# Staging the first expert unit's weights while the attention still runs

## The chip, the cores and the metric

The kernel runs on one core of a Trainium2 chip. The metric is the time of one execution on the device in microseconds (us), the median of several runs. The engines are PE (matrix products), PEld (PE's weight loads), ACT, DVE and POOL (elementwise work), and SP, which only issues DMAs here; POOL issues some DMAs too. Every engine works off its own list of instructions in a fixed order, and a semaphore holds an instruction back until what it reads is there.

## The reference

Three stages follow one another. First a linear attention with a state, for 4 x 8 heads, 768 steps, head width 48:

```
for t in range(S):
    y[:, :, t] = q_t @ state
    state = state + b_t * k_t (x) (v_t - k_t @ state)        # k normalized
```

Its output, as x of 3072 tokens x 384, goes through a mixture of 8 experts. All experts see all tokens and are weighted by P, the softmax of x @ w_gate after 8 rounds of row and column normalization:

```
for e in range(8):
    out += P[:, e:e+1] * (maximum(x @ w1[e], 0) @ w2[e])     # w1: 384 x 1024, w2: 1024 x 384
```

A last stage computes (((x @ u1) * (x @ u2)) @ u3) @ u4. Everything is float32. The kernel gets there with pairs: each operand is split into a rounded high part and the remainder (hi and lo), and a product is three matmuls: hi hi, hi lo, lo hi.

## The kernel before, in words

Every operation is recorded in a plan (`Plan.op`) with its possible engines, a cost, what it reads and writes, and a priority; a smaller number goes first. `Plan.order` then simulates the engines with these costs and emits the program in the order that comes out. An operation that may run on POOL or DVE gets its engine there. The hardware follows that order per engine, and waits where data is late.

The attention runs in 12 chunks (`prep_k`, `invert`, `tt_make`, `prep_q`, `seq`). Expert 0 is computed beside it chunk by chunk (`e0`), from the weights in the eight slots of `wA`. On PE the last chunks of `e0` come after the end of the attention. The normalization of P (`sinkhorn`) runs on DVE between them, with a small PE product in each of its eight rounds.

Experts 1 to 7 follow in `phase_b`. Tokens are taken in three passes of 1024; in a pass every expert is done in two halves of 512 hidden features, so a pass has 14 units (`unit`), and a unit has two pairs q = 0, 1 of 128-feature blocks. The first product of a pair of blocks with two groups of tokens is done by a scheme of the Strassen kind, which needs, beside the blocks of w1 themselves, five sums and differences of them: S1 to S4, kept in the tile `wS`, and S5, kept in place of a block in `wA`. A unit has 66 such matmuls for the two pairs together (the steps of `STEPS`), and then 72 matmuls with w2 into six outputs (`m2`), each multiplied by P on DVE and added to the tile `acc` on POOL.

`load_pair` brings one pair in. In the first pass (p = 0) it loads the raw float32 rows of two blocks with four DMAs into the two buffers of `rawB` (ring `self.rawB`), splits each into hi (ACT) and lo (POOL or DVE) in the pair's two slots of `wA`, forms the five sums in place in `rawB` (`sub`), splits these into `wS` and `wA`, and writes the finished forms to DRAM with two DMAs (`wq_d`, `ws_d`). The later passes load those forms. The sums overwrite the raw rows, so they come after both splits of the raw rows; and since all pairs share the two buffers of `rawB`, the loads of the next pair come after the splits of the sums.

Two gates matter. `w1open` (prio -200) fires when the attention's preparation is done: `open_w1` frees the pool `prep` and opens `ident` and `rawB`. `bopen` fires when all of the attention is done: `open_b` frees its pools and opens `xT` (the tokens' forms), `acc`, `hB`, `wS` and others. The loads into `rawB` carry `r0`, the gate `w1open` and the gate `x11` (the attention's last chunk written to DRAM); the copy into `wS` carries `bopen`. The slots of `wA` that the first unit's pairs go to are 0 to 3, which `e0` reads until its last chunk. `phase_b` calls `load_pair` for the first unit with prio 390 and for unit n + 1 with prio 400.5 + n. `forms` makes the nine forms of a pass's tokens.

Of the kernel before, what the change touches and what calls it, by code (L numbers as in the profile page):

```python
# [6 lines left out]
F32 = mybir.dt.float32  # L7
F32R = mybir.dt.float32r
# [4 lines left out]
ALU = mybir.AluOpType  # L13
# [19 lines left out]
HB = 5  # L33
# [10 lines left out]
BB = 2.0  # L44
# [274 lines left out]
def pool2(n):  # L319
    return (2.2 * n + 70) / 1000  # L320
# [6 lines left out]
def actb(n):  # L327
    return (n / 1.2 + 155) / 1000


def dveb(n, pair=False):
    return (n * (1.25 if pair else 1.0) + 140) / 960


class Kernel:
# [533 lines left out]
            e, self.wb(n)[:, 768:1536], rv(), self.wb(n)[:, 0:768].bitcast(F32), ALU.subtract),  # L869
            r=[(raw, 0), (raw, 1), ("w", sl, 0)], w=[("w", sl, 1)], prio=prio)  # L870

    def load_pair(self, p, e_, h, q, prio):

        nc, g, T, a = self.nc, self.g, self.T, self.a
        r0 = ["w1open", "x11"]
        n1 = 8 * e_ + 4 * h + 2 * q
        ps = 2 * h + q
        wk = lambda n: [("w", n % 8, i) for i in range(2)]
        sk = [("wS", ps, i, m) for i in range(2) for m in range(2)]
        two = lambda: T["wA"][:, n1 % 8:n1 % 8 + 2].rearrange("p a n -> p (a n)")  # L880
        if p:
            self.dma(two, lambda: T["wq_d"][e_, ps], 1572864, [("wq", e_, ps)], wk(n1) + wk(n1 + 1), prio, eng="POOL")
            self.dma(lambda: T["wS"][:, ps], lambda: T["ws_d"][e_, ps], 524288, [("ws", e_, ps)], sk, prio, eng="POOL")
            return
        raws = []
        for j, n in enumerate((n1, n1 + 1)):
            f, sl = n % 8, n % 8
            raw = self.rawB.new()
            raws.append(raw)
            rv = lambda raw=raw: T["rawB"][:, raw.at]  # L890
            self.dma(lambda rv=rv: rv()[:, 0:384].rearrange("p (k f) -> p k f", k=3),
                     lambda f=f: a["moe_w1"][e_, :, 128 * f:128 * f + 128].rearrange("(k p) f -> p k f", p=128), 196608, r0, [(raw, 0)], prio)
            self.dma(lambda rv=rv: rv()[:, 384:768], lambda f=f: a["moe_w2"][e_, 128 * f:128 * f + 128, :], 196608, r0, [(raw, 1)], prio)
            c0 = 128 * j
            m = 768 - c0
            g.op({"ACT": actb(m)}, lambda e, n=n, rv=rv, c0=c0: self.copy("ACT", self.wb(n)[:, c0:768], rv()[:, c0:768]),
                 r=[(raw, 0), (raw, 1)], w=[("w", sl, 0)], prio=prio)
            g.op({"POOL": pool2(m), "DVE": BB * dveb(m, True)}, lambda e, n=n, rv=rv, c0=c0: self.tt(
                e, self.wb(n)[:, 768 + c0:1536], rv()[:, c0:768], self.wb(n)[:, c0:768].bitcast(F32), ALU.subtract),
                r=[(raw, 0), (raw, 1), ("w", sl, 0)], w=[("w", sl, 1)], prio=prio)  # L900
        r1, r2 = raws
        k = lambda raw, i: T["rawB"][:, raw.at, 128 * i:128 * i + 128]

        def sub(out, i0, i1, op, m=1):

            g.op({"POOL": pool2(128), "DVE": BB * dveb(128, True)}, lambda e: self.tt(e, k(*out), k(*i0), k(*i1), op), r=[], w=[(r1, 0), (r2, 0)], prio=prio)
        sl2 = (n1 + 1) % 8
        sub((r2, 1), (r2, 0), (r2, 1), ALU.add)
        sub((r2, 0), (r1, 0), (r2, 0), ALU.subtract)
        sub((r1, 0), (r2, 1), (r1, 0), ALU.subtract)  # L910
        sub((r1, 1), (r1, 1), (r1, 0), ALU.subtract)
        sub((r1, 2), (r1, 2), (r2, 2), ALU.subtract)
        ws = lambda i, c0=0: T["wS"][:, ps, 512 * i + c0:512 * i + c0 + 256]
        rk = [(r1, 0), (r2, 0)]
        for m, src, dst, key in ((256, lambda: T["rawB"][:, r1.at, 0:256], lambda i: ws(i), lambda i: ("wS", ps, i, 0)),
                                 (256, lambda: T["rawB"][:, r2.at, 0:256], lambda i: ws(i, 256), lambda i: ("wS", ps, i, 1)),
                                 (128, lambda: T["rawB"][:, r1.at, 256:384], lambda i: self.wb(n1 + 1)[:, 768 * i:768 * i + 128], lambda i: ("w", sl2, i))):
            g.op({"ACT": actb(m)}, lambda e, src=src, dst=dst: self.copy("ACT", dst(0), src()), r=rk + ["bopen"], w=[key(0)], prio=prio)
            g.op({"POOL": pool2(m), "DVE": BB * dveb(m, True)}, lambda e, src=src, dst=dst: self.tt(e, dst(1), src(), dst(0).bitcast(F32), ALU.subtract),
                 r=rk + [key(0)], w=[key(1)], prio=prio)  # L920
        self.dma(lambda: T["wq_d"][e_, ps], lambda: two().bitcast(F32), 1572864, wk(n1) + wk(n1 + 1), [("wq", e_, ps)], 1000)
        self.dma(lambda: T["ws_d"][e_, ps], lambda: T["wS"][:, ps].bitcast(F32), 524288, sk, [("ws", e_, ps)], 1000)

# [206 lines left out]
    def phase_b(self):  # L1130
        nc, g, T, a = self.nc, self.g, self.T, self.a
        self.rawB = Ring(range(2), fifo=True)

        def open_w1(e):
            self.close("prep")
            self.open("wBp", "right", ident=((128, 128), F32))
            self.open("rawp", "right", rawB=((128, 2, 768), F32))
        self.after("w1open", self.prep_ops, -200, open_w1)
        self.dma(lambda: T["ident"], lambda: a["ident"], 65536, ["w1open"], ["ident"], -100)
        self.sinkhorn()  # L1140
        self.after("x11", [g.wr["xs", 11, b] for b in range(2)], -200)

        def open_b(e):
            self.close("xst")
            self.close("seq")
            self.open("xTp", "left", xT=((128, 4, 2, 4, 3, 128), F32R))
            self.open("accp", "left", acc=((128, 2, 3, 512), F32))
            self.open("hBp", "right", hB=((128, HB, 1024), F32R), wS=((128, 4, 1024), F32R))
            self.open("cvp", "right", cv=((128, 3, CN), F32R), cvr=((128, 1, 2 * CN), F32), rt=((128, 4, 512), F32))
            self.open("pbp", "right", pb=((128, 2, 512), F32), tmp=((128, 2, 512), F32))  # L1150
        self.hringB = Ring([], fifo=True)
        self.rt = Ring([], fifo=True)

        def opened(end):
            self.hringB.free.extend([(end, i) for i in range(HA, HA + HB)])
            self.rt.free.extend([(end, i) for i in range(4)])
        self.after("bopen", self.seq_ops + self.prep_ops, -200, open_b, hook=opened)
        self.after("hA", self.e0_ops, -200, hook=lambda end: self.hringB.free.extend([(end, i) for i in range(HA)]))
        self.spread_p()
        units = [(p, e_, h) for p in range(3) for e_ in range(1, NE) for h in range(2)]  # L1160
        for n, (p, e_, h) in enumerate(units):
            pr = 400.0 + n
            if n == 0:
                for q in range(2):
                    self.load_pair(p, e_, h, q, 390)
            if (e_, h) == (1, 0):
                self.forms(p, pr - .6)
            if h == 0:
                pb = [self.pbring.new() for _ in range(2)]
                for s in range(2):  # L1170
                    self.dma(lambda s=s, pb=pb: T["pb"][:, pb[s].at], lambda s=s, e_=e_, p=p: T["p_d"][
                        e_, 512 * self.PASSES[p][s]:512 * self.PASSES[p][s] + 512].partition_broadcast(128), 262144, ["pd"], [pb[s]], pr - .4)
            if n + 1 < len(units):
                for q in range(2):
                    self.load_pair(*units[n + 1], q, pr + .5)
            self.unit(p, e_, h, pr, 250.0 + n / 100, pb)
            if n == NC0:
                self.after("cv0", [g.wr["acc", 0, 2]], 2)
            if (e_, h) == (4, 0):
                self.add_first(p, pr + .6)  # L1180
            if (e_, h) == (7, 1) and p < 2:
                for s, ch in enumerate(self.PASSES[p]):
                    self.dma(lambda ch=ch: T["xf_d"][ch], lambda s=s: T["acc"][:, s], 786432, [("acc", s, kk) for kk in range(3)], [("xf", ch)], 260 + n / 100)
# [300 lines left out]
```

## Time and profile before

| | us |
|---|---|
| time, median of 3 runs | 2138.53 (2131.8 to 2141.47) |
| the profiled execution's own time | 2133.49 |
| span of that execution, first to last instruction | 2131.3 |
| PE busy in it | 2034.6 (95%) |
| DVE, POOL, ACT busy | 1245.0, 843.3, 712.8 |

The profile is of one execution. Times in its rows are microseconds from the start of the span. A busy share says nothing about which engine sets the end in a stretch; for that the stretch itself is read, with what each engine waited for. L368 is the line of the helper that issues every two-input elementwise operation, L361 that of every copy on ACT, L357 that of the matmuls, L388 that of the DMAs, so the rows are told apart by their tiles; b is a PSUM bank, y_d and w_d stand for the DRAM tensors with a number in their name.

### The profile page before, as it was taken

The numbers are of one execution on the slowest core, as the hardware profiler recorded it, in microseconds if no ns is written. First come the engines' busy times: TensorE is split into PE (matmuls) and PEld (weight loads), VectorE is DVE, ScalarE is ACT, GpSimd is POOL, SyncE is SP. The second block draws the span as 40 slices with busy tenths as digits, with TensorE's granted clock in tenths as the row PEclk, the third lists the DMA queues.
The fourth block names the chain that finished last, engine by engine and source line by source line (L and its number), as shares of the span: only waits on it lengthen the run. The fifth ranks groups of instructions, "written<-read, shape, count | busy, mean of one in ns | idle before, by whom it ended". The sixth has DMA issues, their size and how long they took to land.

```text
span 2131.3 us, 39119 instructions
## 1 busy us (share of the span) xinstructions
PE 2034.6 (95%) x16017; PEld 1734.2 (81%) x16017; DVE 1245.0 (58%) x1950; ACT 712.8 (33%) x1384; POOL 843.3 (40%) x903
## 2 busy tenths in 40 slices
PE   2899999989999999999999999999999999999999
PEld 1798889968887788788887888788877888988888
DVE  7998883535445545757667667666667644222222
ACT  3543333234334344333233234233232232222222
POOL 3101100246676766735547545434555534200000
PEclk9899999999999999999999999999999999999999
DMA  6523332155556565766565555555565455510000
GB/s 215 160 83 109 97 99 73 53 190 214 187 189 202 189 216 197 252 218 213 177 212 187 186 191 197 198 202 193 177 219 186 163 167 174 113 34 27 16 18 27
DMA packets 165460, 331.60 MB, mean 156 GB/s; under 512 B 13280, under 2 KB 117664, under 8 KB 153760
## 3 DMA queue, kind: packets, MB, share of 16 engines
q1 hardware_dynamic: 131392, 193.82, 27.6%
q0 software_dynamic: 33888, 135.28, 18.8%
q8 instruction: 126, 2.06, 0.4%
q14 instruction: 54, 0.44, 0.1%
HBM read 235.10 MB, written 93.95 MB: 154 GB/s over the span
## 4 chain that ended last, share of the span: by engine, by line
PE 79%; DVE 7%; DMA 5%; POOL 4%; issue 3%; ACT 1%; SPq 1%; DVEq 0%; POOLq 0%; ACTq 0%
PE b L357 79%; DMA rawB<-in_moe_w 2%; DVE prod L368 1%; SPq L388 1%; POOL wA L368 1%; DMA kt<-in_kT 1%; POOL acc L368 1%; DVE cv L371 1%; POOL rawB L368 1%; POOL wS L368 1%; DVE b L368 1%; DVE hA L371 0%; DMA w_d<-cv 0%; DVE t L568 0%; DMA wA<-wq_d 0%
## 5 line engine op out<-in xcount | busy, mean ns | idle before, releaser
L357 PE MATMUL b<-hA,wA 128*128 128x512 f32 (+1 forms) x2367 | 505.4, 353 | 7.6 <-DVE hA L371 7.5
L357 PEld LDWEIGHTS b<-hA,wA 128*128 128x128 f32 x2367 | 390.9, 189 | 70.8 <-DVE hA L371 8.9
L368 POOL TENSOR_TENSOR acc<-acc,tmp 128x512 f32<-128x512 f32 x252 | 331.9, 1319 | 157.5 <-DVE tmp L368 153.5
L357 PE MATMUL b<-hB,wA 128*128 128x512 f32 x1521 | 389.4, 391 | 0.0
L357 PEld LDWEIGHTS b<-hB,wA 128*128 128x128 f32 x1521 | 287.6, 189 | 60.0
L357 PE MATMUL b<-xr,wA 128*128 128x256 f32 (+1 forms) x1620 | 331.0, 338 | 1.5 <-DVE a L371 1.3
L357 PEld LDWEIGHTS b<-xr,wA 128*128 128x128 f32 x1620 | 252.8, 191 | 34.5 <-DVE a L371 1.4
L368 DVE TENSOR_TENSOR tmp<-b,pb 128x512 f32<-128x512 f32 x234 | 161.0, 689 | 204.2 <-PE b L357 189.5
L361 ACT ACTIVATE rt<-b 128x512 f32<-128x512 f32 x300 | 178.2, 597 | 253.4 <-PE b L357 247.2
L357 PE MATMUL b<-xT,wA 128*128 128x512 f32 x1008 | 253.4, 392 | 8.1 <-ACT wA L361 6.8
L368 DVE TENSOR_TENSOR b<-b,rt 128x512 f32<-128x512 f32 x252 | 173.6, 695 | 119.7 <-ACT rt L361 63.8
L357 PEld LDWEIGHTS b<-xT,wA 128*128 128x128 f32 x1008 | 190.0, 189 | 50.1 <-ACT wA L361 7.2
L357 PE MATMUL b<-xT,wS 128*128 128x512 f32 x756 | 202.2, 393 | 9.6 <-ACT rt L361 5.3
L368 POOL TENSOR_TENSOR cv<-cv 128x256 f32<-128x256 f32 (+2 forms) x177 | 129.1, 729 | 190.6 <-DVE cv L1246 111.4
L371 DVE SCALAR_TENSOR_TENSOR hA<-b,hA 128x512 fp32r<-128x512 f32 x215 | 144.3, 687 | 63.5 <-ACT hA L1056 38.0
L357 PEld LDWEIGHTS b<-xT,wS 128*128 128x128 f32 x756 | 141.7, 189 | 44.3 <-ACT rt L361 7.7
L368 DVE TENSOR_TENSOR rt<-b,rt 128x512 f32<-128x512 f32 x48 | 33.2, 692 | 186.0 <-PE b L357 186.0
L371 DVE SCALAR_TENSOR_TENSOR hB<-b,hB 128x512 fp32r<-128x512 f32 x169 | 115.4, 686 | 34.4 <-ACT hB L1056 33.9
L1056 ACT ACTIVATE hB<-b 128x512 fp32r<-128x512 f32 x169 | 100.4, 596 | 100.5 <-DVE b L368 98.4
L368 POOL TENSOR_TENSOR wA<-rawB,wA 128x768 fp32r<-128x768 f32 (+2 forms) x66 | 96.1, 1462 | 89.5 <-ACT wA L361 88.7
L361 ACT ACTIVATE cv<-cv 128x256 fp32r<-128x256 f32 x72 | 29.1, 405 | 269.2 <-DVE cv L371 269.2
L1056 ACT ACTIVATE hA<-b 128x512 fp32r<-128x512 f32 x167 | 97.0, 597 | 50.8 <-DVE b L368 28.8
(164 smaller groups left out, 2357.6 us busy)
## 6 DMA issues: line engine op xcount, KB each, us to landing
wA<-wq_d POOLq DMA_DIRECT2D x56, 1536.0 KB, 8.9
wq_d<-wA SPq DMA_DIRECT2D x28, 1536.0 KB, 7.4
wS<-ws_d POOLq DMA_DIRECT2D x56, 512.0 KB, 5.0
rawB<-in_moe_w SPq DMA_DIRECT2D x112, 192.0 KB, 4.4
ws_d<-wS SPq DMA_DIRECT2D x28, 512.0 KB, 3.0
w_d<-cv SPq DMA_DIRECT2D x112, 128.0 KB, 2.1
pb<-p_d SPq DMA_DIRECT2D x42, 256.0 KB, 4.4
cvr<-in_w3T SPq DMA_DIRECT2D x32, 256.0 KB, 2.7
```

The source lines that it names most:

```text
L357: self.nc.tensor.matmul(*args, skip_group_check=True, **kw)
L361: self.nc.scalar.activation(out=out, in_=in_, func=AF.Copy, **({} if scale is None else {"scale": scale}))
L368: self.E[eng].tensor_tensor(out=out, in0=in0, in1=in1, op=op)
L371: self.nc.vector.scalar_tensor_tensor(out=out, in0=in0, scalar=scalar, in1=in1, op0=op0, op1=op1)
L388: return self.g.op({eng: cost}, lambda _: e.dma_start(out=out(), in_=in_()), r=r, w=w, prio=prio, nbytes=nbytes, lat=lat)
L1056: g.op({"ACT": actb(512)}, lambda e: nc.scalar.activation(out=hv(0), in_=self.ps(s, 512), func=AF.Relu), r=[s], w=[(out, 0, 0)], prio=pe)
```

## The change

`load_pair` gets a parameter `early`. The first unit's first pair loads into `rawB` as before; the second pair loads with early=True into `acc[:, 0]`, which has the size of two raw buffers, through a ring of its own. The loads of both pairs wait for `w1open` alone and no longer for `x11`. The writes of `acc[:, 0]` by the first unit are ordered in the plan behind all operations of the second pair (key `raw1`), its two stores to DRAM among them.

The sums no longer overwrite the raw rows. They go to a new tile `sums` (128 x 640), S1 to S4 under one key and S5 under another, for all pairs of the first pass. They read the raw rows only, so the plan lets them come before, between or after the splits into `wA`. The split into `wS` is one copy and one subtraction of 512 columns where it was two of each with 256; it no longer reads `bopen`. There is one `sums` tile for all pairs.

`sums`, `wS` and `acc` are opened by `open_w1`, on the right side, where `wS` and `acc` were opened by `open_b`, `acc` on the left side. The tiles that `open_b` opens on the right side come to lie at other addresses.

```diff
-    def load_pair(self, p, e_, h, q, prio):
+    def load_pair(self, p, e_, h, q, prio, early=False):
-        r0 = ["w1open", "x11"]
+        r0 = ["w1open"] if (p, e_, h) == (0, 1, 0) else ["w1open", "x11"]
...
+        ring = Ring(range(2), fifo=True) if early else self.rawB
+        rawv = lambda raw: T["acc"][:, 0].rearrange("p k n -> p (k n)")[:, 768 * raw.at:768 * raw.at + 768] if early else T["rawB"][:, raw.at]
...
-            g.op({"POOL": pool2(128), "DVE": BB * dveb(128, True)}, lambda e: self.tt(e, k(*out), k(*i0), k(*i1), op), r=[], w=[(r1, 0), (r2, 0)], prio=prio)
-        sub((r2, 1), (r2, 0), (r2, 1), ALU.add)
-        sub((r2, 0), (r1, 0), (r2, 0), ALU.subtract)
-        sub((r1, 0), (r2, 1), (r1, 0), ALU.subtract)
-        sub((r1, 1), (r1, 1), (r1, 0), ALU.subtract)
-        sub((r1, 2), (r1, 2), (r2, 2), ALU.subtract)
+        L = lambda m: lambda: T["sums"][:, 128 * m:128 * m + 128]
+        rk = [(raw, i) for raw in raws for i in range(2)]
+            g.op({"POOL": pool2(128), "DVE": BB * dveb(128, True)}, lambda e: self.tt(e, L(m)(), i0(), i1(), op), r=rk,
+                 w=["sums5" if m == 4 else "sums"], prio=prio)
+        sub(3, k(r2, 0), k(r2, 1), ALU.add)
+        sub(2, k(r1, 0), k(r2, 0), ALU.subtract)
+        sub(0, L(3), k(r1, 0), ALU.subtract)
+        sub(1, k(r1, 1), L(0), ALU.subtract)
+        sub(4, k(r1, 2), k(r2, 2), ALU.subtract)
+        for m, src, dst, key, keys in ((512, lambda: T["sums"][:, 0:512], ws, "sums", [[("wS", ps, i, y) for y in range(2)] for i in range(2)]),
+                                       (128, L(4), s5, "sums5", [[("w", sl2, i)] for i in range(2)])):
-            g.op({"ACT": actb(m)}, ..., r=rk + ["bopen"], w=[key(0)], prio=prio)
+            g.op({"ACT": actb(m)}, ..., r=[key], w=keys[0], prio=prio)
...
-            self.open("rawp", "right", rawB=((128, 2, 768), F32))
+            self.open("rawp", "right", rawB=((128, 2, 768), F32), sums=((128, 640), F32))
+            self.open("wSp", "right", wS=((128, 4, 1024), F32R))
+            self.open("accp", "right", acc=((128, 2, 3, 512), F32))
-            self.open("accp", "left", acc=((128, 2, 3, 512), F32))
-            self.open("hBp", "right", hB=((128, HB, 1024), F32R), wS=((128, 4, 1024), F32R))
+            self.open("hBp", "right", hB=((128, HB, 1024), F32R))
...
-                for q in range(2):
-                    self.load_pair(p, e_, h, q, 390)
+                self.load_pair(p, e_, h, 0, 390)
+                m = len(g.ops)
+                self.load_pair(p, e_, h, 1, 390, True)
+                self.after("raw1", g.ops[m:], -200)
+                g.op({"CTL": 0.0}, lambda e: None, r=["raw1"], w=[("acc", 0, kk) for kk in range(3)], prio=-200)
```

## Rows read from the trace of the kernel before

**Rows 1.** Profile page, first part: busy time, share of the span, instructions.

```profile
PE 2034.6 (95%) x16017; PEld 1734.2 (81%) x16017; DVE 1245.0 (58%) x1950; ACT 712.8 (33%) x1384; POOL 843.3 (40%) x903
```

**Rows 2.** Stretches: length, busy PE, PEld, DVE, ACT, POOL; granted clock, DMA share, GB/s.

```profile
356.00:388.00 32.00, 32.00 (x321) 31.48 (x320) 6.92 (x11) 8.70 (x17) 0.00 (x0) 1.00 0.41 118
436.40:438.90 2.50, 0.00 (x0) 0.00 (x0) 1.39 (x2) 1.01 (x3) 2.22 (x5) 1.00 0.96 293
448.40:456.40 8.00, 7.21 (x19) 4.92 (x20) 2.11 (x4) 4.22 (x10) 7.03 (x9) 0.60 0.14 59
463.24:479.56 16.32, 16.32 (x74) 13.51 (x73) 4.31 (x7) 3.96 (x7) 8.83 (x11) 1.00 0.42 145
462.00:900.00 438.00, 427.52 (x1857) 348.88 (x1856) 235.19 (x336) 172.79 (x332) 300.11 (x322) 0.99 0.59 204
```

**Rows 3.** Timeline of PE: start, length, operation, count, idle time before and releaser.

```profile
433.90 2.41 PE L357 MATMUL b<-xT,wA 128*128 128x512 f32 x9
438.95 2.05 PE L357 MATMUL b<-xT,wS 128*128 128x512 f32 x6 [2.64 <-ACT wS L361]
448.47 1.22 PE L357 MATMUL b<-xT,wA 128*128 128x512 f32 x2 [6.77 <-ACT wA L361]
450.41 3.35 PE L357 MATMUL b<-xT,wA 128*128 128x512 f32 x7 [0.73 <-POOL wA L368]
463.24 0.84 PE L357 MATMUL b<-hB,wA 128*128 128x512 f32 x3
```

**Rows 4.** Timeline of SP's DMA issues, in the same columns.

```profile
356.53 0.43 SPq L388 DMA_DIRECT2D ident<-in_ident  x1
363.52 2.08 SPq L388 DMA_DIRECT2D rawB<-in_moe_w  x4
391.82 23.93 SPq L388 DMA_DIRECT2D y_d<-yr  x6
440.31 3.90 SPq L388 DMA_DIRECT2D rawB<-in_moe_w  x4
```

**Rows 5.** Tile rawB: its sums on POOL, duration min/median/max in ns; its DMAs' landing.

```profile
L368 POOL TENSOR_TENSOR rawB<-rawB x114: 452/461/634, 436.4 to 869.8; 128x128 f32<-128x128 f32 x114
DMA to landing us min/median/max: 2.4/4.4/8.1
```

**Rows 6.** Timeline of ACT.

```profile
386.41 0.84 ACT L361 ACTIVATE xr<-xst 128x768 fp32r<-128x768 f32 x1 [2.64 <-PE b L357]
431.58 1.47 ACT L361 ACTIVATE wA<-rawB 128x768 fp32r<-128x768 f32 x2
438.48 0.72 ACT L361 ACTIVATE wS<-rawB 128x256 fp32r<-128x256 f32 x2 [0.73 <-POOL rawB L368]
```

**Rows 7.** Timeline of POOL.

```profile
388.38 1.29 POOL L368 TENSOR_TENSOR rt<-xT 128x512 f32<-128x512 f32 x1 [63.30 <-DVE xr L368]
398.61 2.67 POOL L368 TENSOR_TENSOR xT<-xT 128x512 fp32r<-128x512 f32 x2 [7.59 <-ACT xT L361]
432.50 3.82 POOL L368 TENSOR_TENSOR wA<-rawB,wA 128x768 fp32r<-128x768 f32 x2 [1.08 <-ACT wA L361]
438.98 1.48 POOL L368 TENSOR_TENSOR wS<-rawB,wS 128x256 fp32r<-128x256 f32 x2
```

**Rows 8.** Timeline of DVE.

```profile
368.60 0.96 DVE L368 TENSOR_TENSOR xr<-xst,xr 128x768 fp32r<-128x768 f32 x1 [2.80 <-ACT xr L361]
398.88 1.24 DVE L371 SCALAR_TENSOR_TENSOR p<-p,cs 128x192 f32<-128x192 f32 x1
408.88 0.35 DVE L371 SCALAR_TENSOR_TENSOR p<-p,cs 128x192 f32<-128x192 f32 x1
882.54 4.93 DVE L368 TENSOR_TENSOR xr<-xT,xr 128x512 fp32r<-128x512 f32 x1
```

**Rows 9.** Timeline of PE in the rest of the first pass.

```profile
714.17 2.01 PE L357 MATMUL b<-xT,wS 128*128 128x512 f32 x6 [1.48 <-ACT wS L361]
888.13 0.61 PE L357 MATMUL b<-hA,wA 128*128 128x512 f32 x1 [3.99 <-DVE hA L371]
```

More of the change, by code (lines that the diff above doesn't have):

```diff
@@ L885, in load_pair @@
         raws = []
+        ring = Ring(range(2), fifo=True) if early else self.rawB
+        rawv = lambda raw: T["acc"][:, 0].rearrange("p k n -> p (k n)")[:, 768 * raw.at:768 * raw.at + 768] if early else T["rawB"][:, raw.at]
         for j, n in enumerate((n1, n1 + 1)):
             f, sl = n % 8, n % 8
-            raw = self.rawB.new()
+            raw = ring.new()
             raws.append(raw)
-            rv = lambda raw=raw: T["rawB"][:, raw.at]
+            rv = lambda raw=raw: rawv(raw)
             self.dma(lambda rv=rv: rv()[:, 0:384].rearrange("p (k f) -> p k f", k=3),
@@ L901, in load_pair @@
         r1, r2 = raws
-        k = lambda raw, i: T["rawB"][:, raw.at, 128 * i:128 * i + 128]
-        def sub(out, i0, i1, op, m=1):
-            g.op({"POOL": pool2(128), "DVE": BB * dveb(128, True)}, lambda e: self.tt(e, k(*out), k(*i0), k(*i1), op), r=[], w=[(r1, 0), (r2, 0)], prio=prio)
+        k = lambda raw, i: lambda: rawv(raw)[:, 128 * i:128 * i + 128]
         sl2 = (n1 + 1) % 8
-        sub((r2, 1), (r2, 0), (r2, 1), ALU.add)
-        sub((r2, 0), (r1, 0), (r2, 0), ALU.subtract)
-        sub((r1, 0), (r2, 1), (r1, 0), ALU.subtract)
@@ L911, in load_pair @@
-        sub((r1, 1), (r1, 1), (r1, 0), ALU.subtract)
-        sub((r1, 2), (r1, 2), (r2, 2), ALU.subtract)
[L913 to L918, printed above, removed]
+        L = lambda m: lambda: T["sums"][:, 128 * m:128 * m + 128]
@@ new lines, in load_pair, with sub @@
+        ws = lambda i: T["wS"][:, ps, 512 * i:512 * i + 512]
+        s5 = lambda i: self.wb(n1 + 1)[:, 768 * i:768 * i + 128]
+        rk = [(raw, i) for raw in raws for i in range(2)]
+        def sub(m, i0, i1, op):
+            g.op({"POOL": pool2(128), "DVE": BB * dveb(128, True)}, lambda e: self.tt(e, L(m)(), i0(), i1(), op), r=rk,
+                 w=["sums5" if m == 4 else "sums"], prio=prio)
+        sub(3, k(r2, 0), k(r2, 1), ALU.add)
+        sub(2, k(r1, 0), k(r2, 0), ALU.subtract)
@@ new lines, in load_pair @@
+        sub(0, L(3), k(r1, 0), ALU.subtract)
[3 more added lines that the diff above has]
+                                       (128, L(4), s5, "sums5", [[("w", sl2, i)] for i in range(2)])):
+            g.op({"ACT": actb(m)}, lambda e, src=src, dst=dst: self.copy("ACT", dst(0), src()), r=[key], w=keys[0], prio=prio)
@@ L919, in load_pair @@
             g.op({"POOL": pool2(m), "DVE": BB * dveb(m, True)}, lambda e, src=src, dst=dst: self.tt(e, dst(1), src(), dst(0).bitcast(F32), ALU.subtract),
-                 r=rk + [key(0)], w=[key(1)], prio=prio)
+                 r=[key] + keys[0], w=keys[1], prio=prio)
         self.dma(lambda: T["wq_d"][e_, ps], lambda: two().bitcast(F32), 1572864, wk(n1) + wk(n1 + 1), [("wq", e_, ps)], 1000)
```

## The prediction

> **What bounds the kernel now.** I read the page's busy times first: PE is busy 95% of the span [rows 1]. So only two things can move the time: stretches in which PE stands still, and stretches in which it runs slowly. The windows show where the change works [rows 2]. From 356 to 388 us PE is full, while POOL does nothing and ACT works 8.70 of 32 us. From 436.4 to 438.9 PE does nothing. From 448.4 to 456.4 it runs at a granted clock of 0.60, that is, largely at the lower of its levels 1.2 and 2.4 GHz. From 463.24 to 479.56 it is full again at 1.00: the first unit's 72 matmuls with w2 in 16.32 us, 0.2267 us each.
>
> PE's timeline names the waits [rows 3]. At 433.90, as the expert-0 work ends, the first unit's products begin. They stop for 2.64 us until ACT has written `wS` for the first pair, for 6.77 us until ACT has split the second pair's first rows, and for 0.73 us until POOL has. That is 10.14 us of waiting. After the 6.77 us PE comes back at half rate: seven matmuls take 3.35 us, where at 0.2267 us they would need some 1.7.
>
> Why the second pair is late stands in SP's timeline [rows 4]. The first four loads go out at 363.52, the second four only at 440.31, because both need `rawB`, and the first pair's sums hold it until its last split, which begins on POOL at 438.98 [rows 7].
>
> **The change, part by part.**
>
> *The first unit's products.* They now take from 433.90 to 463.24 = 29.34 us. There are 66 (3 + 6 + 3 + 6 + 3 + 6 + 6 for each pair); at 0.2267 us they need 14.96. So 14.38 us is the most that can go here: 10.14 of waits, the rest half rate and short waits inside the groups. With the change both pairs' raw rows and `wS` are ready long before 433.9. What remains behind the end of expert 0 are the splits into slots 0 to 3, which expert 0 frees one by one; ACT starts on slot 0 at 431.58 and needs 1.47 us for two slots [rows 6]; POOL starts at 432.50 and needs 3.82 for two [rows 7], 1.91 each.
>
> Is POOL late then? If all four go to POOL, they end at 434.4, 436.3, 438.2 and 440.1. PE needs slot 0 at 434.3 (third matmul) and does nine matmuls on it, then six with S2 and S1 of pair 0, which need `wS` alone: to about 437.7. Then three on slot 1 (ready since 436.3), to 438.4; then nine on slot 2 (438.2), six with `wS`, and at about 441.8 three on slot 3 (440.1). Each split is there 0 to 1.7 us before its use. What is late next is slot 2, by little. If some go to DVE, it is earlier. I take 1.2 us of remaining waits. From below the bound is 0.2, the wait for slot 0 that is there now. From above it is 5.4: three splits of token forms at 1.29 and the 1.48 us of S5's work [rows 7], the nearest forms, put ahead of slot 2 on POOL. No drop of the clock comes with that, since the wait of 2.64 was followed by six matmuls in 2.05 us, at most a third longer than full rate gives, and only the 6.77 by half rate [rows 3]. Term: -14.4 + 1.2 = -13.2 us (bounds -14.2 and -9.0).
>
> *The early loads, sums and splits.* Eight loads are issued on SP right behind the load of `ident` at 356.53, where four were at 363.52; four issues cost 2.08 us [rows 4]. Queued behind them on SP are the attention's last stores and reload, whose result ACT splits only at 386.41, when PE releases it [rows 6], more than 20 us after the loads, so a few us there cost nothing. POOL gets ten sums at 0.461 us [rows 5] and two splits of 512 columns at 1.29 [rows 7], 7.2 us in all, in a stretch where it had nothing to do for 63.3 us before 388.38 [rows 7]. ACT gets two copies of 512 columns, each under 0.74, the mean of the two larger ones at 431.58 [rows 6]. All of this lies beside a full PE.
>
> It is not free in one respect. The plan counts 0.66 us of transfer and 0.9 of latency per load; the trace has 4.4 us to landing, 8.1 at most [rows 5]. So the ACT copies may stand in ACT's order 2 to 4 us ahead of their data, and behind them are the relus of expert 0 that PE waits for. A copy that is 3 us late costs PE perhaps 1 to 2, since ACT is idle more than two thirds of that stretch. I take +1.0 us for both pairs (bounds -0.5, as instructions leave the stretch after 434; and +6, 3 us for each pair).
>
> Against this change speaks a rule too. DVE's p<-p,cs takes 0.35 us alone and 1.24 while POOL works (the first of two POOL operations from 398.61), and late in the pass a DVE subtraction of 512 columns takes 4.93 us [rows 7, 8]. The Trainium skill, "SBUF — State Buffer", section "SBUF: two separate sides", says that DVE operations with two SBUF inputs and POOL's share a port pair that one holds for a whole instruction while the other is blocked; the rows agree. By it, sums that fell into the normalization of P, after 390, would cost some 0.9 us a round; I expect them done by about 380, so the sum stays as it is.
>
> What DVE does meet there is the split of a chunk into `xr` (0.96 us at 368.60 [rows 8]), and PE's logits wait for it; one POOL operation of 1.29 ahead of it is within the bound.
>
> *The other pairs of the first pass.* Nothing moves in number of DMAs. Per pair two ACT copies of 256 (0.72 together) become one of 512 (under 0.74), and two POOL splits of 256 (1.48) one of 1.29 [rows 6, 7]; off PE's path. More important: sums need not wait for the raw rows' splits, and `rawB` is free sooner by the splits of the sums, about 1.48 us and S5's. PE stands still for 438.0 - 427.52 = 10.5 us between 462 and 900 [rows 2], among it 1.48 at 714.17 for `wS`, which this removes, and 3.99 at 888.13 for an `hA` that DVE wrote late [rows 9], which it does not touch by itself. The new order of POOL and DVE can move such stalls either way. I take the one row that answers: -1.5 us. The bounds are -6 (half of the idle time) and +6 (one stall of the 3.99 us kind, with some half rate behind it). Passes 2 and 3 load the same finished forms: 0.
>
> *Moved tiles.* `hB`, `rt`, `pb`, `tmp` come to lie over attention tiles that are dead before 388; their first uses are not earlier than that: 0 us.
>
> *Sum:* -13.2 + 1.0 - 1.5 = -13.7 us. From the profiled execution's 2133.49 this gives 2119.8. That execution is 5.0 us under the median of the three, 2138.53, from which the sum gives 2124.8. The mean of these four is 2136.3. I go from there: 2136.3 - 13.7 = 2122.6, in round figures 2123.
>
> **The rivals.**
>
> *The splits into `wA` take the stall's place.* For it: ACT and POOL can't start before expert 0 frees the slots, and POOL's 1.9 us per slot is more than half of what PE takes for a pair's first nine matmuls. Against it: the reckoning above, and DVE works little then. If slots 2 and 3 come last, 5.4 us stay: 2122.6 + 4.2 = 2127.
>
> *ACT stalls expert 0.* Each early copy waits its full 3 us in front of a relu, so PE loses 6 instead of 1: 2128. For it: the landing of 4.4 to 8.1 us against the plan's reckoning. Against it: ACT is idle 23 of the 32 us [rows 2], so most relus would not stand right behind a waiting copy.
>
> *The early loads are not early.* If the plan puts the second four behind a store on SP that waits for expert 0, such as the six that took 23.93 us from 391.82 [rows 4], they land by 420, and sums and splits run into the tail. `wS` of pair 1 is then ready at about 428, still before its use at 440. Only if they also miss that does it stay near what it was: 2132 to 2137. Little speaks for it, as nothing is ahead of them on SP at 357 but `ident`.
>
> *Slower: one `sums` tile for all pairs.* The next pair's sums wait for the last split from `sums`, in POOL's order, and behind them on POOL are the sums into `acc`, behind these on DVE the two `tmp` buffers, behind these PE's w2 outputs. 26 pairs follow the first two. If each costs PE 1.0 us, that is 26 us: 2122.6 + 26 = 2149. It beats the gain from 13.7 / 26 = 0.53 us per pair on. Against it: a unit takes some 31 us, so a pair has 15.6, and in between the raw rows have to be loaded, 4.4 us; POOL is busy 300 of 438 us [rows 2].
>
> **How the numbers follow.** Forecast 0.68, splits late 0.13, ACT stall 0.09, not early 0.04, one tile 0.06. Less than 0.5% (10.7 us, to 2127.8 from the median) can't be told from no change here. The forecast's own range, 2113 to 2131, holds more than 0.5% in about 0.83 of its cases, 0.57; the splits and the ACT stall, at 2127 and 2128, in a third of theirs, 0.07. Faster 0.64. Slower by more than 0.5% is the one-tile case in two thirds, 0.04. The rest, 0.32, is the same. The range: from 2136.3 with the best bounds together about 2115, and 3 us for the runs' spread, 2112; upwards to the other cases at 2127 to 2137, of which I keep most: 2136.
>
> **What would show it.** Right: eight raw loads on SP between 357 and 366, POOL's ten sums and two splits before 388, PE's 66 first products in 15 to 17 us with no wait over 1.5, the clock at 1.00 through 456, the w2 products beginning 12 to 14 us sooner. Wrong: a wait on `wA` over 3 us at about 438; ACT's copies waiting for POOL between 360 and 375 with PE idle there; waits between units on `wS` or `tmp` that add up to more than now. If the transition is gone from PE's timeline and the time is still the same, the gain was given back in the first pass, and the third term was wrong.

## The result, and the profile after

The changed kernel takes 2113.02 us (median of 4 runs, 2105.79 to 2120.65), the kernel before in the same comparison 2139.76 (4 runs, 2131.80 to 2141.47): a ratio of 0.9883 on record (the medians alone give 0.9875), 95% interval 0.984 to 0.9926. A second comparison gave 2117.63 (6 runs) against 2135.73 (14 runs): 0.9912, 0.9893 to 0.993. So the gain is about 18 to 27 us; the forecast was 13.7, to 2123.

The page of the changed kernel, busy time by engine, beside [rows 1]: PE's share has risen by one point.

```profile
PE 2025.7 (96%) x16017; PEld 1731.0 (82%) x16017; DVE 1230.1 (58%) x1935; ACT 708.2 (34%) x1355; POOL 847.2 (40%) x891
```

Stretches of the changed kernel, in the columns of [rows 2]: the end of the attention from the same place of the program on (SP issues `ident`'s load at 352.24 here, at 356.53 before), the first unit's products, and the stretch from the first of them to DVE's first `acc<-b,pb` of the second pass, which holds the whole first pass (the first unit of a pass writes `acc` directly, the others go through `tmp`).

```profile
352.00:384.00 32.00, 30.80 (x307) 29.80 (x307) 6.58 (x9) 8.48 (x17) 8.80 (x13) 1.00 0.58 175
431.27:449.54 18.27, 17.78 (x77) 13.85 (x76) 14.42 (x20) 11.90 (x23) 12.72 (x12) 1.00 0.98 347
431.27:897.04 465.77, 459.52 (x2022) 378.67 (x2021) 245.65 (x356) 186.85 (x338) 320.52 (x329) 1.00 0.60 216
```

The same last stretch in the kernel before:

```profile
433.90:922.25 488.35, 467.65 (x2016) 379.73 (x2015) 256.89 (x371) 192.00 (x368) 321.68 (x350) 0.98 0.61 210
```

The two spans, 2131.3 and 2104.0, differ by 27.3 us. Of these, 4.29 lie ahead of `ident`, where the program is the same: chance of that execution. From `ident` to the first product it is 77.37 before and 79.03 after: +1.66. From there to the second pass it is 488.35 and 465.77: -22.58. The rest, some -2, is behind. So the change gave about 20.9 us there.

PE's timeline of the changed kernel, where [rows 3] stood before:

```profile
431.27 2.40 PE L357 MATMUL b<-xT,wA 128*128 128x512 f32 x9
433.50 1.52 PE L357 MATMUL b<-xT,wS 128*128 128x512 f32 x6
...
438.11 1.66 PE L357 MATMUL b<-xT,wS 128*128 128x512 f32 x6 [0.37 <-ACT rt L361]
...
446.82 2.88 PE L357 MATMUL b<-xT,wA 128*128 128x512 f32 x12
449.54 0.84 PE L357 MATMUL b<-hB,wA 128*128 128x512 f32 x3
```

The 10.14 us of waits are gone, and so is the half rate. The longest wait is 0.37. The plan now puts nine products of the next unit ahead of the first w2 product, so that 75 instead of 66 lie before it: at 0.2267 us they need 17.0, and the stretch is 18.27. For the same reason the first w2 product comes only 11 us sooner after the first product (18.27 against 29.34).

SP's timeline of the changed kernel, beside [rows 4]: all eight raw loads are out by 358.9, with two stores of `xst` among them.

```profile
352.24 0.43 SPq L388 DMA_DIRECT2D ident<-in_ident  x1
352.72 1.98 SPq L388 DMA_DIRECT2D rawB<-in_moe_w  x4
354.81 0.38 SPq L388 DMA_DIRECT2D acc<-in_moe_w  x1
355.29 1.78 SPq L388 DMA_DIRECT2D xs_d<-xst  x2
357.12 1.76 SPq L388 DMA_DIRECT2D acc<-in_moe_w  x3
```

The price stands in the timeline of all engines of the changed kernel just behind these loads:

```profile
358.18 1.30 POOL L368 TENSOR_TENSOR sums<-rawB 128x128 f32<-128x128 f32 x3 [36.31 <-DMA rawB<-in_moe_w]
...
360.48 0.63 ACT L361 ACTIVATE wS<-sums 128x512 fp32r<-128x512 f32 x1 [2.93 <-POOL sums L368]
...
364.42 0.63 ACT L361 ACTIVATE wS<-sums 128x512 fp32r<-128x512 f32 x1 [2.83 <-POOL sums L368]
364.96 0.83 ACT L361 ACTIVATE xr<-xst 128x768 fp32r<-128x768 f32 x1
...
365.82 1.40 DVE L368 TENSOR_TENSOR xr<-xst,xr 128x768 fp32r<-128x768 f32 x1 [3.50 <-ACT xr L361]
...
365.84 0.53 PE L357 MATMUL b<-xr,wg 128*16 128x256 f32 x3 [0.29 <-ACT xr L361]
...
367.28 0.53 PE L357 MATMUL b<-xr,wg 128*8 128x256 f32 x3 [0.91 <-DVE xr L368]
```

Each copy of sums stands in ACT's order before its data are there: ACT waits 2.93 and 2.83 us. Right behind the second is the copy of the last chunk but one into `xr`, for which the logits wait. It begins 12.72 us behind `ident`'s load, where it was 11.19 before. DVE's half of it takes 1.40 beside POOL's split at 365.13, where it took 0.96 [rows 8], and PE stands 0.29 and 0.91 us.

In the rest of the first pass three stalls are left. PE's timeline of the changed kernel:

```profile
662.86 0.96 PE L357 MATMUL b<-xr,wS 128*128 128x512 f32 x3 [1.67 <-ACT rt L361]
...
666.18 0.96 PE L357 MATMUL b<-xT,wS 128*128 128x512 f32 x3 [0.99 <-ACT rt L361]
...
862.25 0.73 PE L357 MATMUL b<-xr,wA 128*128 128x512 f32 x2 [3.09 <-DVE xr L368]
```

### The profile page after: what moved, and what is told of

It is laid out like the page before. It is cut to its first block, busy times and chain, and to the rows that moved or that the text cites. A ratio compares the mean times of both kernels' runs of the same rounds, so it can differ in the third digit from the quotient of the medians.

```text
span 2104.0 us, 39081 instructions
## 1 busy us (share of the span) xinstructions
PE 2025.7 (96%) x16017; PEld 1731.0 (82%) x16017; DVE 1230.1 (58%) x1935; ACT 708.2 (34%) x1355; POOL 847.2 (40%) x891
## 4 chain that ended last, share of the span: by engine, by line
PE 75%; DVE 3%; DMA 2%; issue 1%; POOL 1%; ACT 1%; SPq 0%; DVEq 0%; POOLq 0%; ACTq 0%
PE b L357 75%; DMA wA<-wq_d 1%; DMA wo_d<-cv 1%; DVE cv L371 1%; DVE xr L368 0%; DVE b L368 0%; POOL acc L368 0%; POOL cv L368 0%; DVE hA L371 0%; DMA rawB<-in_moe_w 0%; POOL tmp L368 0%; POOL wA L368 0%; ACT rt L361 0%; DVE tmp L368 0%; DMA w_d<-cv 0%
## 5 line engine op out<-in xcount | busy, mean ns | idle before, releaser
L368 POOL TENSOR_TENSOR cv<-cv 128x256 f32<-128x256 f32 (+3 forms) x171 | 124.9, 730 | 197.7 <-DVE cv L1254 114.3
L368 POOL TENSOR_TENSOR wA<-rawB,wA 128x768 fp32r<-128x768 f32 (+1 forms) x53 | 91.1, 1729 | 31.8 <-ACT wA L361 27.2
```

What stands on the lines that cost most here:

```text
L368: self.E[eng].tensor_tensor(out=out, in0=in0, in1=in1, op=op)
```

## The experiments

Two measures are used for every kernel: from `ident`'s load to the first product (the early work's price), and from there to the second pass (the gain). For the latter, "lost" is what groups of 128x512 products (the rows of PE's timeline) take to the next group's start beyond 0.2267 us per product, where that is over 0.25 us; it is divided at the first w2 product, and the last 45 us of the pass, where the forms for the second pass are made, stand apart.

| kernel | ident to first product | first product to second pass | lost in first unit | lost in rest, without end | at the end |
|---|---|---|---|---|---|
| before | 77.37 | 488.35 | 14.15 | 10.5 | 5.7 |
| before again | 77.37 | 489.29 | 14.86 | 9.6 | 6.3 |
| changed | 79.03 | 465.77 | 0.94 | 3.0 | 3.3 |
| changed again | 79.33 | 467.68 | 1.11 | 2.9 | 4.9 |
| first unit only | 79.30 | 473.53 | 0.94 | 7.8 | 6.4 |
| sums' tile only | 77.37 | 479.47 | 12.75 | 2.9 | 4.9 |
| loads early, sums late | 77.39 | 474.99 | 8.55 | 2.95 | 4.9 |
| copies planned later | 78.56 | 468.18 | 0.52 | 2.9 | 6.0 |
| sums behind splits | 83.37 | 468.98 | 1.34 | 4.5 | 5.2 |
| raw rows held | 79.19 | 466.68 | 1.02 | 3.0 | 5.1 |
| both | 78.94 | 478.53 | 1.12 | 17.6 | 0.9 |
| copies on POOL, P in `rawB` | 77.37 | 466.18 | 0.53 | 3.3 | 4.9 |
| the same, forms on POOL | 77.34 | 468.79 | 1.04 | 2.95 | 7.4 |
| the same, for the last pass only | 77.36 | 464.97 | 1.00 | 3.3 | 3.3 |

**Before and changed, once more.** No edit.

> The kernel before, unchanged, for a second trace: how much of the difference between the two profiles is the execution and not the program. Both theories: up to the issue of ident's load (356.5 us before, 352.2 after) the two programs are the same, so that point should scatter by some 4 us here too. PE's lost time (what its 128x512 products take beyond 0.2267 us each) should come out as in the first trace: about 14 us from the first product of the first unit to the end of that unit's 66, and about 16 us in the rest of the first pass. If the lost time of the first pass scatters by more than 3 us, the part of the gain that lies there is not the program's.

> The changed kernel, unchanged, for a second trace and more times. Expected: 0.984 to 0.993 of the kernel before; lost time on PE about 1.3 us in the first unit's products and about 6 us in the rest of the first pass, within 2 us, and 1.2 us of waits of PE at about 365 us behind ACT and DVE.

Before took 2138.34 us (one run), the changed kernel 2117.63 (above). Both stretches repeat: 77.37 twice before, 79.03 and 79.33 after, and a gain of 22.58 and 21.61 us. PE's timeline of the kernel before, repeated, shows the stall that the changed kernel has at 662.86 and 666.18, longer:

```profile
683.60 0.96 PE L357 MATMUL b<-xr,wS 128*128 128x512 f32 x3 [1.97 <-ACT rt L361]
...
688.22 0.97 PE L357 MATMUL b<-xT,wS 128*128 128x512 f32 x3 [2.28 <-ACT rt L361]
```

**The change divided in two.** First the early staging alone (`sums_apart` holds the changed kernel's sums, `sums_in_place` those of before, for every other pair):

```diff
+        if (p, e_, h) == (0, 1, 0):
+            self.sums_apart(raws, rawv, n1, ps, prio)
+        else:
+            self.sums_in_place(raws, n1, ps, prio)
```

> The early loads, early sums and the moved tiles for the first unit's two pairs; all later pairs form their sums in place in rawB and split them in two halves, as before. Theory A (the 10 us in the rest of the first pass come from the separate sums tile, which lets wS be ready earlier and frees rawB earlier): the first unit's products lose about 1.3 us as in the changed kernel, but the rest of the first pass loses some 14 to 18 us as before, so the time is some 12 to 14 us under the kernel before, ratio about 0.994. Theory B (those 10 us come from the new order and the head start as such, whatever the sums do): the rest of the first pass loses about 6 us here too, ratio about 0.989.

Then the sums' tile and the piece of 512 alone, for all pairs, with the loads, the second pair's place and `wS` as before:

```diff
-        r0 = ["w1open"] if (p, e_, h) == (0, 1, 0) else ["w1open", "x11"]
+        r0 = ["w1open", "x11"]
...
-                self.load_pair(p, e_, h, 0, 390)
...
-                self.load_pair(p, e_, h, 1, 390, True)
...
+                for q in range(2):
+                    self.load_pair(p, e_, h, q, 390)
```

> The separate sums tile and the split in one piece for all pairs, but nothing early: the second pair loads into rawB after the first, wS and acc are opened where they were before, and all loads wait for the attention's last store. Theory A: the first unit's products lose some 11 to 14 us (the second pair's loads can start only about 2 us sooner), the rest of the first pass loses about 6 us, so the time is some 10 to 13 us under the kernel before, ratio about 0.995. Theory B: the rest of the first pass loses some 16 us as before; ratio 0.998 to 1.000.

The first took 2126.96 us, 0.9958 of before (0.9938 to 0.9977); the second 2121.97, 0.9941 (0.9922 to 0.9961). The two parts together, 0.42% and 0.59%, are about the 0.88% of the whole change in that comparison. The first has the short transition and, with 14.2 us lost behind it (15.9 to 16.2 before), nearly the old first pass (PE's timeline):

```profile
673.65 0.98 PE L357 MATMUL b<-xr,wS 128*128 128x512 f32 x3 [1.97 <-ACT rt L361]
...
677.93 0.96 PE L357 MATMUL b<-xT,wS 128*128 128x512 f32 x3 [1.91 <-ACT rt L361]
```

The second has the old transition (PE's timeline; the seven products at 448.80 take half rate again) and the new first pass, 2.9 us lost:

```profile
446.90 1.22 PE L357 MATMUL b<-xT,wA 128*128 128x512 f32 x2 [4.32 <-ACT wA L361]
448.80 3.19 PE L357 MATMUL b<-xT,wA 128*128 128x512 f32 x7 [0.67 <-POOL wA L368]
```

The intervals of the two overlap, so the times don't say which part is the larger. By the stretches from `ident` to the second pass the first gains 13.4 us and the second 9.4 (552.8 and 556.8, against 566.2, the mean of the two traces of before). So the part that the prediction had put at 1.5 us brought some 9, a little under half of the gain. In the second `wS` and `acc` lie where they were, so this part doesn't need their new places.

**Are early loads enough?** The first unit's sums wait for expert 0; its raw rows come early as in the changed kernel.

```diff
-        rk = [(raw, i) for raw in raws for i in range(2)]
+        rk = [(raw, i) for raw in raws for i in range(2)] + (["hA"] if (p, e_, h) == (0, 1, 0) else [])
```

> The changed kernel, but the first unit's sums wait until expert 0 is done; its raw rows still arrive during the attention. Theory C (the gain at the transition needs the sums early too): ten sums at 0.46 us and two splits of 1.29 us on POOL, plus two ACT copies, now stand beside the four splits into wA between 432 and 445, so PE loses 4 to 8 us in the first unit's products instead of 1.3. Rival (early loads alone do it, the sums find room): 1.3 to 3 us. The rest of the first pass loses 3 to 6 us as in the changed kernel, and the 1.7 to 2.0 us that the stretch from ident's load to the first product grew by are gone (77.4 us instead of 79.0 to 79.3).

No: 8.55 us are lost in the first unit, a little more than the 4 to 8 expected, and it took 2119.70 us (one run). The sums run on POOL behind the splits into `wA`, at 440.84, and PE waits for `wS` in its timeline:

```profile
439.39 1.89 PE L357 MATMUL b<-xT,wA 128*128 128x512 f32 x7 [1.41 <-POOL wA L368]
...
444.06 0.73 PE L357 MATMUL b<-xT,wS 128*128 128x512 f32 x2 [2.78 <-ACT wS L361]
```

Of the 13.5 us between before (14.5, the mean of both) and the changed kernel (1.0), the early loads bring 6.0 and the early sums 7.5. The attention takes 77.39 without the early sums: its +1.7 comes from them, not from the loads.

**Where do the 1.7 us come from?** The plan is told that the eight early loads land 4 us later.

```diff
+        lat = 4.0 if (p, e_, h) == (0, 1, 0) else 0.0
...
-                      ... 196608, r0, [(raw, 0)], prio)
+                      ... 196608, r0, [(raw, 0)], prio, lat=lat)
```

> The changed kernel, with 4 us more of reckoned latency for the first unit's eight loads, so that the plan puts the two ACT copies into wS and POOL's sums later in their engines' orders; nothing else is edited. Theory D (the stretch from ident's load to the first product grew from 77.4 to 79.0 to 79.3 us because ACT stood 2.9 us in front of each copy, and POOL's work beside DVE's split of the chunk): it comes back to 77.4 to 78.0 us, and the time is 1 to 2 us under the changed kernel, ratio to the kernel before about 0.990. Rival (it is the DMA traffic of eight loads beside the attention's stores): it stays at 79.

78.56 us: only some 0.6 of the 1.8 came back, and the time, 2115.43 (0.9887, 0.9849 to 0.9925), can't be told from the changed kernel's. The expectation of 77.4 to 78.0 was missed. The copies still wait; only another chunk is behind them (timelines of ACT and PE):

```profile
382.32 0.63 ACT L361 ACTIVATE wS<-sums 128x512 fp32r<-128x512 f32 x1 [1.80 <-POOL sums L368]
...
386.86 0.63 ACT L361 ACTIVATE wS<-sums 128x512 fp32r<-128x512 f32 x1 [2.37 <-POOL sums L368]
...
387.81 0.61 PE L357 MATMUL b<-masks,yr 16*128 16x8 f32 x4 [1.11 <-ACT yr L361]
```

So it isn't the landing alone: with it allowed for, the copy still stands in ACT's order ahead of the end of POOL's sums.

**What of the sums' tile brings the gain of the first pass?** Two things became free. Sums no longer wait until both raw rows are split into `wA`, and `rawB` no longer waits for the splits of the sums. Each freedom is taken away alone, for all pairs but the first unit's:

```diff
+        rk = [...] + ([] if (p, e_, h) == (0, 1, 0) else wk(n1) + wk(n1 + 1))
```

> The changed kernel, but for all pairs except the first unit's the sums are made to wait for both raw rows' splits into wA, as they had to in place; the separate tile, the split in one piece and the earlier release of rawB stay. Theory E (the rest of the first pass gains because wS is ready earlier): its lost time goes back to 9 to 16 us. Theory F (it gains because rawB is free sooner and the next loads start earlier): it stays at 3 to 6 us.

```diff
-                 r=[key] + keys[0], w=keys[1], prio=prio)
+                 r=[key] + keys[0] + ([] if (p, e_, h) == (0, 1, 0) else rk), w=keys[1], prio=prio)
```

> The changed kernel, but for all pairs except the first unit's the two buffers of rawB are held until the sums are split, as before; the sums may still come before the splits into wA. Theory E: the lost time of the rest of the first pass stays at 3 to 6 us. Theory F: it goes back to 9 to 16 us. If both this and the kernel with the sums after the splits stay low, the piece of 512 columns or the new order as such is left.

Neither alone gives much back: 4.5 us lost with the sums behind the splits (2.9 to 3.0 in the changed kernel, 9.6 to 10.5 before), and 3.0 with the raw rows held. The theory of the early release of `rawB` fell, and that of the early sums explains 1.5 of some 7 us. The times were 2124.76 and 2120.71 (one run each). Part of the first one's is an accident in the attention: its plan changed there too, ACT's first copy waited 4.53, PE 1.88, and PE went on at half rate. Timelines of ACT and PE, and the stretch:

```profile
372.36 0.63 ACT L361 ACTIVATE wS<-sums 128x512 fp32r<-128x512 f32 x1 [4.53 <-POOL sums L368]
...
377.71 0.53 PE L357 MATMUL b<-xr,wg 128*16 128x256 f32 x3 [1.88 <-ACT xr L361]
```

```profile
362.00:400.00 38.00, 35.22 (x322) 34.06 (x321) 7.38 (x11) 9.71 (x19) 9.07 (x13) 0.91 0.49 148
```

The granted clock of 0.91 is part of it at the lower level, 1.2 GHz; that is why the price here is 83.37 - 77.37 = 6.0 us, more than PE's waits of 1.88 and 0.90.

Then both were taken away at once, to learn if either is enough:

```diff
+        late = (p, e_, h) != (0, 1, 0)
...
-            ... r=rk,
+            ... r=rk + (wk(n1) + wk(n1 + 1) if late else []),
...
-                 r=[key] + keys[0], w=keys[1], prio=prio)
+                 r=[key] + keys[0] + (rk if late else []), w=keys[1], prio=prio)
```

> The changed kernel, but for all pairs except the first unit's the sums wait for both rows' splits and rawB is held until the sums are split, so the order of the work is the one that sums in place force; only the separate tile and the split in one piece of 512 columns remain. Lost time of the first pass behind the first unit, without the end of the pass, was 10.5 and 9.6 us in the two traces of the kernel before, 3.0 and 2.9 in the changed kernel, 4.5 with the late sums alone and 3.0 with the held rows alone. Theory G (either freedom is enough, and with both gone the gain goes): 8 to 11 us here. Rival (the gain is the single piece of 512 columns and the order it brings): 3 to 5 us.

The gain of the first pass is gone: with the end of the pass 18.5 us are lost, before 15.9 to 16.2, and the time is 2133.82 us (one run). So with the piece of 512 either freedom suffices. But without the end it is 17.6, where 8 to 11 had been expected. PE waits three times for `wS`, each time for ACT's copy and then for POOL's remainder, 6.0 us in all, where before has one such wait of 1.48 (0.92 in the repeat). Two of the three stand here (its timeline):

```profile
716.68 0.73 PE L357 MATMUL b<-xT,wS 128*128 128x512 f32 x2 [0.65 <-ACT wS L361]
718.03 1.19 PE L357 MATMUL b<-xT,wS 128*128 128x512 f32 x4 [0.62 <-POOL wS L368]
...
751.43 0.74 PE L357 MATMUL b<-xT,wS 128*128 128x512 f32 x2 [1.44 <-ACT wS L361]
```

Six more of PE's waits, again 6.0 us, are for ACT's `rt`. Ahead of each of these `rt` copies in ACT's order stands the copy of the sums, and it waits 1.28 to 3.69 us for them, as in the first unit. The first of the six and the longest (ACT's timeline; PE waits 0.84 and 2.64 us behind them):

```profile
548.79 0.63 ACT L361 ACTIVATE wS<-sums 128x512 fp32r<-128x512 f32 x1 [1.75 <-POOL sums L368]
...
679.57 0.63 ACT L361 ACTIVATE wS<-sums 128x512 fp32r<-128x512 f32 x1 [3.69 <-DVE sums L368]
```

So the surplus is late sums and copies that wait for them in front of what PE needs. Whether two pieces of 256 with the sums' tile would wait less was not run and stays open.

**A version that beats both.** The early copies go to POOL, behind the sums that they wait for, and the two broadcasts of P for expert 0 in each of the passes 2 and 3 into `rawB`, which is empty then. In a second kernel the subtractions of the token forms are POOL's alone; in a third only those for the last pass.

```diff
-            g.op({"ACT": actb(m)}, ...
+            g.op({"POOL": pool1(m)} if m == 512 and (p, e_, h) == (0, 1, 0) else {"ACT": actb(m)}, ...
...
-            b = self.rt.new()
+            b = self.rawB.new() if p else self.rt.new()
...
-        both = {"POOL": pool2(512), "DVE": dveb(512, True)}
+        both = {"POOL": pool2(512)} if p == 2 else {"POOL": pool2(512), "DVE": dveb(512, True)}
```

> The same without the third edit: the forms' remainders go to POOL or DVE by the plan as before. Expected: the first two places as in the version with all three, the ends of the passes as in the changed kernel (3 to 5 us each), 5 to 9 us under the changed kernel.

> A version meant to beat the changed kernel, with three edits whose places are apart: the first unit's two early copies into wS run on POOL instead of ACT; in passes 2 and 3 the two broadcasts of P for expert 0 lie in rawB, which is unused then, instead of in two of the four rt buffers; the remainders of the token forms run on POOL alone. Expected if the readings are right: from ident's load to the first product 77.4 to 78.4 us instead of 79.0 to 79.3 (DVE's split of the chunk still meets POOL); the waits of PE for ACT's rt at about 1105 to 1140 and 1555 to 1590 us, 4.8 and 4.5 us, mostly gone; the waits of 3 to 5 us at the ends of the passes (DVE 5 to 6 us behind POOL) gone. Together 8 to 15 us under the changed kernel, ratio about 0.986. If POOL alone can't do the forms in time, the pass ends lose more, not less.

> The version with the first unit's early copies on POOL and the broadcasts in rawB, and the forms' remainders on POOL alone for the third pass only: at the end of the first pass POOL alone made PE lose 7.2 us instead of 3.3 to 5.2, at the end of the second pass it removed 5.1. Expected: from ident's load to the first product 77.4 us; about 4 to 5 us lost at the end of the first pass; no wait of PE at about 1305 to 1325; 2 to 4 us under the version with all forms on POOL in the trace, ratio to the kernel before 0.982 to 0.985.

They took 2111.79 us (4 runs; 0.9859, 0.9814 to 0.9905), 2106.24 (4 runs; 0.9839, 0.9799 to 0.9879) and 2101.20 (6 runs, 2097.80 to 2108.12; 0.9826, 0.9797 to 0.9854). None was compared with the changed kernel directly, and some of the intervals overlap; but from `ident` to the end of the span the third takes 1743.0 us in its trace, the changed kernel 1751.8 and 1755.7, before 1774.8 and 1775.5. The copies on POOL bring the attention back to 77.34 to 77.37 in all three, the whole price. The two copies take 0.61 and 1.22 there (the first, in POOL's timeline of the third kernel):

```profile
366.43 0.61 POOL L363 CAST wS<-sums 128x512 fp32r<-128x512 f32 x1
```

The broadcasts' new place did not remove the waits for `rt` as expected, it mostly exchanged them: in the second pass of the third kernel PE waits 1.58 us for DVE's `tmp` (1.79 in the first). In the first kernel the second pass takes 448.5 us, as in the changed one (448.5 and 449.4); only the third pass is shorter, 422.8 against 425.4 and 426.2 (to DVE's last `tmp<-b,pb`). The forms on POOL alone remove the wait of 3.5 us and the half rate behind it at the end of the second pass, but at the end of the first they make one (PE's timeline of the second kernel), so that the third has them for the last pass only:

```profile
866.51 0.80 PE L357 MATMUL b<-hA,wA 128*128 128x512 f32 x1 [4.61 <-DVE hA L371]
```

The end of the second pass, in the changed kernel and in the third:

```profile
1290.00:1350.00 60.00, 56.51 (x243) 46.30 (x242) 41.19 (x59) 22.72 (x43) 32.71 (x34) 0.97 0.64 228
```

```profile
1290.00:1350.00 60.00, 60.00 (x266) 49.56 (x265) 47.23 (x66) 23.38 (x45) 38.13 (x37) 1.00 0.65 236
```

## Why the prediction was right, and where it was not

*The first unit's products: right.* Predicted -13.2, measured 0.94 - 14.15 = -13.2, and about -13.7 in the repeat. The working holds in its steps too. It let POOL end the four splits 0.5, 2.4, 4.3 and 6.2 us after PE's first product; POOL's timeline of the changed kernel has them end, two and two, at about 2.0 and 5.8:

```profile
429.87 3.38 POOL L368 TENSOR_TENSOR wA<-rawB,wA 128x768 fp32r<-128x768 f32 x2 [1.08 <-ACT wA L361]
433.21 3.87 POOL L368 TENSOR_TENSOR wA<-acc,wA 128x768 fp32r<-128x768 f32 x2
```

Remaining losses were put at 1.2 and are 0.94 to 1.11. The rival of the late splits is refuted by the longest wait of 0.37, that of loads which are not early by SP's timeline. One reading under its bounds does not hold: that the clock doesn't drop behind a wait of 2.64 us. In the repeat of the kernel before, six products behind a wait of 2.67 us take 2.68 us, at a granted clock of 0.56 (443.15 to 445.83).

*The early work: right in mechanism, a little too small.* Predicted +1.0, measured +1.66 and +1.96. ACT's copies do stand 2.8 to 3.2 us ahead of their data in the two traces, as the step said. The step put relus of expert 0 behind them; what PE waited for, 1.2 us, was the split of the last chunk but one, which it had named only for a meeting with POOL. That is the ACT stall among its rivals, in a small measure. With the copies on POOL the price is zero: ACT's copy into `xr` is then no longer late, and DVE's half meets less of POOL too (1.05 to 1.14 us, not 1.40). So ACT's order is the cause of the late start; how much of the price the 0.44 us of DVE's longer half had by themselves can't be told apart. The rival with 6 us came true in one variant, the sums behind splits.

*The other pairs of the first pass: this step failed.* It was predicted at -1.5, with a lower bound of -6; measured are 6.24 and 7.81 us lost in the rest of the pass, against 16.15 and 15.94, so some -9, outside its bound. Two things went wrong in "I take the one row that answers". First, the step counted the idle time, 10.5 us in [rows 2], and took half of it for the bound (that is 5.3, not 6); but the loss was 16, with short pauses and with products at the lower clock behind two of the waits (granted 0.67 from 679.5 to 684.6 and 0.61 from 888.1 to 892.5). Second, only the wait that names `wS`, 1.48 at 714.17 [rows 9], was taken as touched. With the short pauses around it that place lost 2.6 us, and it is gone; but the waits for ACT's `rt` in the eighth unit, from 676 to 684, 5.2 us with what followed, became 3.0, and the end of the pass, counted from the wait at 872 on, went from 6.9 to 3.3 (4.9 in the repeat). These waits name ACT or DVE, yet they fell when the sums could be done earlier or the raw rows be loaded earlier, and came back when neither could be. The prediction had named both freedoms and given them no price. ACT's order shows a part of the way. The second of the two waits for `rt` in the eighth unit of the kernel before is for a copy that stands behind a split of raw rows, and that waits 3.31 us for their load (3.29 in the repeat; ACT's timeline of the kernel before):

```profile
682.80 0.84 ACT L361 ACTIVATE wA<-rawB 128x768 fp32r<-128x768 f32 x1 [3.31 <-DMA rawB<-in_moe_w]
```

With both freedoms gone it was the copies of late sums that stood there. How the plan turns each freedom into less waiting for `rt` at every place wasn't followed.

*The wait of 3.99 us at the end of the pass* was said to be untouched. It became 3.09 at another operation, of the same kind: DVE's subtraction of 512 columns took 4.93 [rows 8] and takes 5.97 now. DVE's timeline of the changed kernel, while POOL works without a gap:

```profile
856.22 5.97 DVE L368 TENSOR_TENSOR xr<-xT,xr 128x512 fp32r<-128x512 f32 x1
```

```profile
854.15 1.31 POOL L368 TENSOR_TENSOR rt<-xT,rt 128x512 f32<-128x512 f32 x1
855.41 1.29 POOL L368 TENSOR_TENSOR xT<-rt,xT 128x512 fp32r<-128x512 f32 x1
856.66 1.28 POOL L368 TENSOR_TENSOR rt<-xT 128x512 f32<-128x512 f32 x1
857.91 2.51 POOL L368 TENSOR_TENSOR xT<-xT 128x512 fp32r<-128x512 f32 x2
860.39 1.25 POOL L368 TENSOR_TENSOR rt<-xT,rt 128x512 f32<-128x512 f32 x1
```

It ends at 862.19, when POOL's last of these ends at 861.64. This agrees with what the Trainium skill, "SBUF — State Buffer", section "SBUF: two separate sides", states: a DVE operation with two SBUF inputs and a POOL operation that reads SBUF exclude each other. By these rows DVE stood through several of POOL's operations, not through one. The early sums were done ahead of the normalization of P, as predicted, and its operations take what they took: 1.24 and 1.22 us for the first two, 0.35 to 0.36 for the others.

*The slower rival, one `sums` tile for all pairs,* is refuted: with the tile alone the first pass loses less, 2.9 and 4.9 us against 9.6 to 10.5 and 5.7 to 6.3.

*The sum.* With the measured terms it is -13.5 + 1.8 - 9, about -20.7, beside -18 and -27 from the medians and the forecast's -13.7. The forecast was in the right direction; its third term was six times too small. Its range, 2112 to 2136, held the first time, 2113.0, by 1 us and the second, 2117.6, by more: the lower end had 3 us for the runs' spread in it, and without them the first would have lain outside.

## What to carry to other kernels

What a stall costs is read from how long the products take, the slow ones behind a wait included, and not from idle time alone. A change that takes a dependency away between buffers acts on every repetition, also where the wait in the trace names another engine: price each freedom by taking it away alone and both together. Where an instruction stands in an engine's fixed order ahead of its data, look at what stands behind it; here it cost nothing once it ran on the engine that makes the data.

## What was not expected of the hardware

The spread of the times comes mostly from ahead of the change, in the attention. SP issued `ident`'s load, up to which the program does the same in all these kernels, between 352.24 us (changed) and 371.98 (copies planned later). The stretch from 150 to 300 us in these two executions:

```profile
150.00:300.00 150.00, 146.49 (x3880) 133.72 (x3880) 131.33 (x199) 59.02 (x137) 19.08 (x14) 1.00 0.36 108
```

```profile
150.00:300.00 150.00, 143.12 (x3406) 130.41 (x3406) 114.92 (x164) 54.01 (x125) 19.30 (x14) 0.87 0.31 93
```

The granted clock is 1.00 in one and 0.87 in the other, and 12% fewer matmuls were done. Why the clock is lower in the one isn't known. For a change of 1%, that is why stretches from a common point on tell more than two spans.
